# The first block of the last stage ordered by hand, in a fused attention, soft mixture and gated MLP kernel

## The chip, the cores and the metric

The kernel runs on one core of one Trainium2 chip. The metric is the device time of one execution in microseconds (us). A median over runs is given together with the lowest and the highest run. The profile is one further execution with the hardware profiler on.

## The reference

Three layers follow each other. The change lies in the third alone.

```python
# 1: attention with rotary embedding, 4 x 8 heads, 576 tokens, 64 wide -> x of 2304 x 512
attn = softmax(rotate(q) @ rotate(k).T / 8) @ v
# 2: soft mixture of 8 experts with 4 slots each; c: softmax over the 32 slots
x = c @ slot_out                       # c 2304 x 32, slot_out 32 x 512
# 3: MLP, 512 -> 2048 -> 512
h = x @ w_in
out = (h * (1.0 / (1.0 + np.exp(-h)))) @ w_out
```

## The kernel before

The last stage uses that `x @ w_in` is `c @ (slot_out @ w_in)`: it first makes g, the product of the 32 slot rows with w_in, and then needs only 32 rows of contraction for each hidden value. The 2304 tokens are worked in three blocks j of 768, and the 2048 features in 16 chunks k of 128. For one (j, k) the stage does this:

- `hidden(j, k)`: f0 is a matrix product on TensorE (PE) of a chunk of g (`gs`) with the combine weights `cs`, once for each half i of 384 tokens, into a PSUM tile `hps`. Only two such tiles exist (pool `ps_h`, 2 buffers). f1 is the sigmoid on ScalarE (ACT), f2 the product with h on VectorE (DVE), f3 the rounded part `ghi` on ACT, f4 the rest `glo` on DVE. An `hps` tile is free when its f4 is done.
- `products(j, k, i)`: three matrix products of 512 columns (`wo_hi` by `ghi`, `wo_lo` by `ghi`, `wo_hi` by `glo`) for each of six groups of 128 tokens, summed over k in six PSUM tiles `ops`. So a chunk is 18 products of this kind and two of f0.

In block 0 the stage also prepares what the later blocks use. w_out comes from memory as 64-bit words (`w_out_raw`, three buffers in turn). `narrow` makes 32-bit values of a chunk by one instruction on ACT (L143) and two on DVE (L146, L149); `split_hl` then makes `wo_hi` on ACT and `wo_lo` on GpSimd (POOL). Chunks 0, 3, 6 and 10 were converted earlier. `load_wo` issues the load of a later raw chunk on SyncE (SP), and it has to wait until the conversion has read the chunk that was in the same buffer three loads before. `conv_last` converts in the same way the four parts of the last quarter of w_in. g is made in four parts n of four chunks: `g_product(n)` is 32 small products in an `hps` tile and two copies `gh` and `gl` (ACT, DVE), and `g_copy(n, r)` then spreads one chunk of the part by four small DMAs, issued on SP, into `gs`.

The order on the engines: while `tc.manual_schedule()` is open, instructions stand on each engine as the code is written; when `order.close()` has ended it, a scheduler places them. Before, the hand order ends after the hidden chunk 1 of block 0, and the scheduler places all that follows.

The loop over `seq` runs through the 48 pairs (j, k). In step n it works the six `products` of pair n, and after token group i = 2 the `hidden` of pair n + 2. Small jobs are hung on points of the loop by numbers that are 6 n + i: `G_STEPS` says where `g_product` of parts 1 to 3 stands, and `SPREAD` where the first of the four `g_copy` of each part stands (the next three follow 6 apart).

Of the kernel before, what the change touches and what calls it, by code (L numbers as in the profile page):

```python
# [7 lines left out]
F32 = mybir.dt.float32  # L8
# [3 lines left out]
ACTF = mybir.ActivationFunctionType  # L12
ALU = mybir.AluOpType
# [19 lines left out]
TB = 128 * NI  # L33
# [22 lines left out]
QO = (0, 256, 576)  # L56
QN = (256, 320)

G_STEPS = (5, 25, 49)
LOAD_STEP = 28  # L60
SPREAD = (7, 27, 51)
CONV_AT = (2, 5, 8, 9)


@with_exitstack
def attn_softmoe_mlp_kernel(ctx: ExitStack, tc: tile.TileContext, qk, v, cst, phi, w1, w2, w_in, w_out, out):
    nc = tc.nc
    pe, act, dve, pool, sp = nc.tensor, nc.scalar, nc.vector, nc.gpsimd, nc.sync
# [62 lines left out]
    def load_64(src, wp, tag, name):  # L131
        t = wp.tile([128, 1024], U32, tag=tag, name=name)
        sp.dma_start(out=t, in_=src)
        return t.rearrange("p (n t) -> p n t", t=2)

    def narrow(words, out, wp, name, tag="hw", hw=None):
        o = out.bitcast(U32)
        if hw is None:
            hw = wp.tile([128, words.shape[1]], F32, tag=tag, bufs=1, name=name)
        hi = hw.bitcast(U32)  # L140

        def n0():
            act.activation(out=hw, in_=words.bitcast(F32)[:, :, 1], func=ACTF.Prelu, scale=2.0 ** -112, alpha=2.0 ** 32)  # L143

        def n1():
            dve.tensor_scalar(out=o, in0=hi, scalar1=3, scalar2=None, op0=ALU.logical_shift_left)  # L146

        def n2():
            dve.scalar_tensor_tensor(out=o, in0=words[:, :, 0], scalar=29, in1=o, op0=ALU.logical_shift_right, op1=ALU.bitwise_or)  # L149

        return n0, n1, n2

    raw_w, wf_early = {}, {}

    LATE = [k for k in range(16) if k not in W_OUT_EARLY]

    def load_wo(i):
        if i < len(LATE):
            k = LATE[i]
            raw_w[k] = load_64(w_out[128 * k:128 * k + 128], wa, f"w{i % 3}", f"w_out_raw{k}")  # L160
# [3 lines left out]
    def halves(n, i):  # L164
        t = wa.tile([128, 2, 512], F32, tag=f"w{NWA - 2 + i}", name=f"w_in{n}_{i}")
        w_next.update({(n, 2 * i + k): t[:, k] for k in range(2)})
        return t
# [22 lines left out]
    with tc.manual_schedule():  # L190
        with ExitStack() as t1:
# [505 lines left out]
            for p in range(NPAIR):  # L697
# [9 lines left out]
                if p % 4 == 3 and p < NPAIR - 1:  # L707
                    b = p // 4
# [170 lines left out]
            a, b = rot[0], rot[1] = rotary(0), rotary(1)  # L879
# [65 lines left out]
            t = ps_mx.tile([128, 2, 512], F32, tag="mx", name="u_31")  # L945
# [34 lines left out]
            t = ps_mx.tile([128, 2, 512], F32, tag="mx", name="lt3_ps")  # L980
# [6 lines left out]
        def pool2(name, bufs, space=None, st=ctx, **kw):  # L987
            kw.update({"reuse_waits": "tile"}, **({"space": space} if space else {}))
            return st.enter_context(tc.tile_pool(name=name, bufs=bufs, **kw))
# [35 lines left out]
        op = {}  # L1025
# [82 lines left out]
        order = ExitStack()  # L1108
# [38 lines left out]
        t = ps_h.tile([128, 512], F32, tag="h", name="g0_ps")[:, 0:128]  # L1147
# [12 lines left out]
    g2 = pool2("g2", 2, side=left)  # L1160
# [5 lines left out]
    def narrow_wo(k):  # L1166
        w = wf_early[k] = w2p.tile([128, DM], F32, tag="wf", name=f"wf{k}")
        for f in narrow(raw_w.pop(k), w, w2p, f"hwo{k}"):
            f()

    def split_hl(k, w, eng=pool):
        if k in WO_SLOT:
            t = wa.tile([128, 2, DM], F32R, tag=f"w{WO_SLOT[k]}", name=f"wo_hl{k}")
            wo_hi[k], wo_lo[k] = t[:, 0], t[:, 1]
        elif k == WO_TAB:
            t = p_tab.tile([128, 2, S], F32R, tag="tab", name=f"wo_hl{k}")
            wo_hi[k], wo_lo[k] = t[:, 0, 0:DM], t[:, 1, 0:DM]
        else:
            wo_hi[k] = wo.tile([128, DM], F32R, tag=f"hi{k}", name=f"wo_hi{k}")
            wo_lo[k] = wo.tile([128, DM], F32R, tag=f"lo{k}", name=f"wo_lo{k}")  # L1180
        act.activation(out=wo_hi[k], in_=w, func=ACTF.Copy)
        eng.tensor_tensor(out=wo_lo[k], in0=w, in1=wo_hi[k].bitcast(F32), op=ALU.subtract)

    gt, later = {}, []

    def hidden(j, k, between=None):
        ghi = gp.tile([128, 2, TB // 2], F32R, tag="ghi", name=f"ghi{j}_{k}")
        glo = gp.tile([128, 2, TB // 2], F32R, tag="glo", name=f"glo{j}_{k}")
        t, g = {}, {}

        def f0(i):
            t[i] = ps_h.tile([128, TB // 2], F32, tag="h", name=f"hps{j}_{k}_{i}")
            c0 = TB // 2 * i
            pe.matmul(t[i], lhsT=gs2[k // 8][:, 128 * (k % 8):128 * (k % 8) + 128], rhs=cs[j][:, c0:c0 + TB // 2], start=True, stop=True)  # L1194

        def f1(i):
            g[i] = g2.tile([128, TB // 2], F32, tag="g", name=f"g{j}_{k}_{i}")
            act.activation(out=g[i], in_=t[i], func=ACTF.Sigmoid)  # L1198

        def f2(i):  # L1200
            dve.tensor_tensor(out=t[i], in0=t[i], in1=g[i], op=ALU.mult)  # L1201

        def f3(i):
            act.activation(out=ghi[:, i], in_=t[i], func=ACTF.Copy)  # L1204

        def f4(i):
            dve.tensor_tensor(out=glo[:, i], in0=t[i], in1=ghi[:, i].bitcast(F32), op=ALU.subtract)  # L1207

        if between:
            for f, i in ((f0, 0), (f0, 1), (f1, 0), (f2, 0), (f1, 1), (f2, 1)):  # L1210
                f(i)
            copy = between(0)
            f3(0)
            copy()
            for f, i in ((f4, 0), (f3, 1), (f4, 1)):
                f(i)
        elif j == 0:
            f0(0)
            f1(0)
            f2(0)  # L1220

            def rest():
                for f in (f0, f1, f2):
                    f(1)
                def ahead():
                    if k + 1 in LATE:
                        narrow_wo(k + 1)
                        load_wo(LATE.index(k + 1) + 3)
                    elif k in CONV_AT:
                        conv_last(CONV_AT.index(k))  # L1230

                if k > 1:
                    ahead()
                for f in (f3, f4):
                    for i in range(2):
                        f(i)
                if k == 1:
                    ahead()
                else:
                    split_hl(k, wf_early[k])  # L1240
                if k + 1 in LATE and k in CONV_AT:
                    conv_last(CONV_AT.index(k))

            later.append(rest)
        else:
            for i in range(2):
                for f in (f0, f1, f2, f3, f4):
                    f(i)
        gt[j, k] = ghi.rearrange("p a b -> p (a b)"), glo.rearrange("p a b -> p (a b)")

    def conv_last(k):
        if k % 2 == 0:
            halves(3, k // 2)
        words = raw_in[k // 2][:, k % 2].rearrange("p (n t) -> p n t", t=2)
        for f in narrow(words, w_next[3, k], wa, f"hw3_{k}", "w3"):
            f()
# [16 lines left out]
    def g_copy(n, r):  # L1273
        c0 = 512 * (n % 2) + 128 * r
        for q in range(4):
            sp.dma_start(out=gs2[n // 2][32 * q:32 * q + 32, c0:c0 + 128].bitcast(F32), in_=gfull[n][q // 2][32 * r:32 * r + 32].bitcast(F32))
# [8 lines left out]
    seq = [(j, k) for j in range(NBLK) for k in range(16)]  # L1285
# [26 lines left out]
    for i in (2, 3):  # L1312
        load_wo(i)
    hidden(*seq[1])
    later.pop()()
    order.close()
    extra = {}

    def put(x, f):
        extra.setdefault(divmod(x, NI), []).append(f)  # L1320

    for n in range(1, 4):
        put(G_STEPS[n - 1], lambda n=n: g_product(n))
        for r in range(4):
            put(SPREAD[n - 1] + NI * r, lambda n=n, r=r: g_copy(n, r))
    put(LOAD_STEP, lambda: load_last(1))
    for n, (j, k) in enumerate(seq):
        ghi, glo = gt.pop((j, k))
        for i in range(NI):
            if n or i > 3:  # L1330
                products(j, k, i, ghi, glo)
            t = ops[j, i]
            if (n, i) in extra:
                for f in extra.pop((n, i)):
                    f()
            if i == (2 if n else 4) and n + 2 < len(seq):
                hidden(*seq[n + 2])
            elif i == (3 if n else 5) and later:
                later.pop()()
            if k == 15:  # L1340
                o = g2.tile([128, DM], F32, tag="os", bufs=6, name=f"os{j}_{i}")
                if i % 2:
                    dve.tensor_copy(out=o, in_=t)
                else:
                    act.activation(out=o, in_=t, func=ACTF.Copy)
                r0 = TB * j + 128 * i
                sp.dma_start(out=out[r0:r0 + 128], in_=o)
# [46 lines left out]
```

## Time and profile before

| | us |
|---|---|
| median of 3 runs | 557.17 |
| lowest and highest | 556.64, 558.12 |
| the profiled execution, device time | 557.69 |
| its span in the trace | 555.9 |
| TensorE (PE) busy in it | 539.8 |
| VectorE (DVE), ScalarE (ACT) busy | 314.3, 298.6 |

The last stage begins at about 326 us of the span, block 0 ends near 401, and the last matrix product ends at 551.3. A time of the trace counts from the start of the span. The device time holds 1.8 us more than the span.

### The profile page before, as it was taken

Reading aid. Unit: us, or ns where it says so; the run is one execution under the profiler, and the core shown is the slowest. Engines: PE = TensorE matmul, PEld = TensorE weight load, DVE = VectorE, ACT = ScalarE, POOL = GpSimd, SP = SyncE. Lnnn points to the kernel's source line nnn. Section 1 sums busy time; section 2 is a strip of 40 time slices with the busy share of each in tenths; the row PEclk is TensorE's granted clock in tenths of the full one; section 3 lists DMA queues with packets and bytes.
Section 4 is the critical chain, followed back from the end, with each engine's and each line's share of the span. In section 5 each row is a group of like instructions: output and inputs, shape, how many; then the busy total and the mean of one; then the engine's idle time right before and its main releaser. Section 6 shows DMA issues by size and latency. Waiting matters only on the chain.

```text
span 555.9 us, 15287 instructions
## 1 busy us (share of the span) xinstructions
PE 539.8 (97%) x6283; PEld 436.9 (79%) x6283; DVE 314.3 (57%) x826; ACT 298.6 (54%) x582; POOL 113.0 (20%) x105
## 2 busy tenths in 40 slices
PE   8989999999999999999999999999999999999996
PEld 5767898889888989888863457688888888888885
DVE  5767676766656567654130557886454444544442
ACT  3666767656766566664420357666454443533441
POOL 4475433412334323200000032312000000000000
PEclk9999999999999999999999999999999999999999
DMA  8335777555663685753799976361030000300003
GB/s 329 122 101 195 236 263 250 196 183 182 221 222 125 213 284 185 248 191 107 285 340 380 339 297 215 109 223 39 1 114 0 1 0 1 114 2 0 0 1 114
DMA packets 38721, 89.32 MB, mean 161 GB/s; under 512 B 10598, under 2 KB 13948, under 8 KB 36732
## 3 DMA queue, kind: packets, MB, share of 16 engines
q1 hardware_dynamic: 38652, 88.36, 45.7%
q8 instruction: 49, 0.80, 0.6%
q14 instruction: 20, 0.16, 0.1%
HBM read 78.20 MB, written 7.60 MB: 154 GB/s over the span
## 4 chain that ended last, share of the span: by engine, by line
PE 86%; ACT 7%; DVE 4%; issue 3%; ACTq 0%; DVEq 0%
PE ops L1294 11%; PE ops L1296 11%; PE ops L1295 11%; PE u L431 11%; PE st L398 8%; PE psmx L327 4%; PE st_r L411 3%; PE hps L1194 3%; PE xps L459 3%; ACT e L402 3%; PE l L1011 3%; PE l L1032 3%; ACT relu L335 2%; PE u L425 2%; PE psmx L343 2%
## 5 line engine op out<-in xcount | busy, mean ns | idle before, releaser
L1201 DVE TENSOR_TENSOR hps<-hps,g 128x384 f32<-128x384 f32 x96 | 50.6, 562 | 83.3 <-ACT g L1198 83.2
L1198 ACT ACTIVATE g<-hps 128x384 f32<-128x384 f32 x96 | 43.3, 490 | 86.8 <-PE hps L1194 86.7
L348 DVE CUSTOM_DVE_ANT_0 relu<-psmx,relu 128x288 f32<-128x288 f32 x142 | 59.5, 454 | 43.7 <-ACT e L402 38.0
L402 ACT ACTIVATE e<-st 128x512 f32<-128x512 f32 (+1 forms) x128 | 76.4, 650 | 10.4 <-PE st L398 10.3
L431 PE MATMUL u<-v,e 128*64 128x65 f32 x2048 | 80.1, 224 | 0.3 <-ACT e L402 0.3
L1294 PE MATMUL ops<-wo_hi,ghi 128*128 128x512 f32 x198 | 77.9, 394 | 1.5 <-ACT ghi L1204 1.5
L1296 PE MATMUL ops<-wo_hi,glo 128*128 128x512 f32 x198 | 77.6, 392 | 0.0
L1295 PE MATMUL ops<-wo_lo,ghi 128*128 128x512 f32 x198 | 77.2, 390 | 0.0
L431 PEld LDWEIGHTS u<-v,e 128*64 128x64 f32 x2048 | 70.8, 137 | 6.7 <-issue 2.9
L335 ACT ACTIVATE relu<-psmx 128x576 f32<-128x576 f32 x63 | 41.0, 652 | 49.4 <-PE psmx L327 39.7
L277 POOL TENSOR_TENSOR raw<-raw,tab 128x576 f32<-128x576 f32 x28 | 40.5, 1446 | 113.0 <-DMA raw<-in_qk_dram 71.2
L1207 DVE TENSOR_TENSOR glo<-hps,ghi 128x384 fp32r<-128x384 f32 x96 | 50.1, 553 | 4.6 <-ACT ghi L1204 0.7
L1204 ACT ACTIVATE ghi<-hps 128x384 fp32r<-128x384 f32 x96 | 46.0, 492 | 10.5 <-DVE hps L1201 10.3
L1294 PEld LDWEIGHTS ops<-wo_hi,ghi 128*128 128x128 f32 x198 | 37.2, 188 | 9.4 <-ACT ghi L1204 2.5
L1296 PEld LDWEIGHTS ops<-wo_hi,glo 128*128 128x128 f32 x198 | 37.2, 188 | 8.4 <-DVE glo L1207 0.3
L1295 PEld LDWEIGHTS ops<-wo_lo,ghi 128*128 128x128 f32 x198 | 37.2, 188 | 6.3
L274 POOL TENSOR_TENSOR raw<-raw,tab 128x576 f32<-128x576 f32 x28 | 41.9, 1496 | 0.0
L398 PE MATMUL st<-hi 64*128 64x256 f32 (+1 forms) x256 | 39.2, 300 | 0.0
L398 PE MATMUL st<-lo,hi 64*128 64x256 f32 (+1 forms) x256 | 38.2, 293 | 0.0
L398 PE MATMUL st<-hi,lo 64*128 64x256 f32 (+1 forms) x256 | 38.2, 292 | 0.0
L398 PE MATMUL st<-mq,neg_a 64*128 64x256 f32 (+1 forms) x256 | 38.1, 291 | 0.0
L1294 PE MATMUL ops<-wo_hl,ghi 128*128 128x512 f32 x90 | 35.2, 391 | 0.0
(236 smaller groups left out, 993.6 us busy)
## 6 DMA issues: line engine op xcount, KB each, us to landing
w<-in_w_dram SPq DMA_DIRECT2D x64, 512.0 KB
raw<-in_qk_dram SPq DMA_DIRECT2D x14, 1152.0 KB
w_out_raw<-in_w_out_dram SPq DMA_DIRECT2D x16, 512.0 KB
w_in_raw<-in_w_in_dram SPq DMA_DIRECT2D x12, 512.0 KB
v<-in_v_dram SPq DMA_DIRECT2D x16, 325.0 KB
out_dram<-os SPq DMA_DIRECT2D x18, 256.0 KB
w_in<-w_in SPq DMA_DIRECT2D x8, 256.0 KB
w_in_raw<-in_w_in_dram SPq DMA_DIRECT2D x2, 1024.0 KB
```

Source lines behind the costliest of these rows:

```text
L335: act.activation(out=r, in_=pair[:, :, 0:HS], func=ACTF.Relu)
L348: dve.tensor_tensor_reduce(out=r[:, hd], in0=t[hd], in1=r[:, hd], scale=1.0, scalar=-3.0e38, op0=ALU.add, op1=ALU.max, accum_out=mxs[p % 2 ...
L398: pe.matmul(st[:, hd, 0:n], lhsT=a, rhs=b, start=i == 0, stop=i == 3, skip_group_check=True)
L402: act.activation(out=e[:, :, 0:n], in_=st[:, :, 0:n], func=ACTF.Exp, scale=0.125)
L431: pe.matmul(u[q:q + 64, 2 * i + hd], lhsT=e[:, hd, o:o + 64], rhs=x[:, hd], start=n == 0 and i + hd == 0, stop=n == 4, skip_group_check=True)
L1198: act.activation(out=g[i], in_=t[i], func=ACTF.Sigmoid)
L1201: dve.tensor_tensor(out=t[i], in0=t[i], in1=g[i], op=ALU.mult)
L1204: act.activation(out=ghi[:, i], in_=t[i], func=ACTF.Copy)
L1207: dve.tensor_tensor(out=glo[:, i], in0=t[i], in1=ghi[:, i].bitcast(F32), op=ALU.subtract)
L1294: pe.matmul(t, lhsT=a, rhs=wo_hi[k], start=k == 0, stop=False)
L1295: pe.matmul(t, lhsT=a, rhs=wo_lo[k], start=False, stop=False)
L1296: pe.matmul(t, lhsT=b, rhs=wo_hi[k], start=False, stop=k == 15)
```

## The change

Five things change, all in the last stage. The hand order stays open until step n = 14, so it holds for all of block 0. In `hidden` of block 0 the conversions for the next w_out chunk and for w_in stand behind the work of the whole chunk (f0 to f4 for both halves), and `split_hl` of chunk k stands ahead of it; the former split in two pieces (`later`) is gone. The first chunk's first half is worked in 128 and 256 tokens. `hidden` of the third chunk is written after token group 5 of step 0 and not after group 4. Part 3 of g is made at 55 and spread from 57 (49 and 51 before), and `conv_last` runs with chunks 3, 5, 8, 9.

```diff
-G_STEPS = (5, 25, 49)
+G_STEPS = (5, 25, 55)
-SPREAD = (7, 27, 51)
-CONV_AT = (2, 5, 8, 9)
+SPREAD = (7, 27, 57)
+CONV_AT = (3, 5, 8, 9)
...
         if between:
-            for f, i in ((f0, 0), (f0, 1), (f1, 0), (f2, 0), (f1, 1), (f2, 1)):
-                f(i)
+            a, b = slice(0, 128), slice(128, TB // 2)
+            f0(0)
+            f0(1)
+            for w in (a, b):
+                f1(0, w)
+                f2(0, w)
             copy = between(0)
-            f3(0)
+            f3(0, a)
+            f3(0, b)
             copy()
-            for f, i in ((f4, 0), (f3, 1), (f4, 1)):
-                f(i)
+            f4(0, a)
+            f4(0, b)
+            for f in (f1, f2, f3, f4):
+                f(1)
         elif j == 0:
...
+            if k > 1:
+                split_hl(k, wf_early[k])
+            for f in (f0, f1, f2, f3, f4):
+                for i in range(2):
+                    f(i)
+            if k + 1 in LATE:
+                narrow_wo(k + 1)
+                load_wo(LATE.index(k + 1) + 3)
+            if k in CONV_AT:
+                conv_last(CONV_AT.index(k))
...
     hidden(*seq[1])
-    later.pop()()
-    order.close()
...
-            if i == (2 if n else 4) and n + 2 < len(seq):
+            if i == (2 if n else 5) and n + 2 < len(seq):
+                if n == 14:
+                    order.close()
                 hidden(*seq[n + 2])
-            elif i == (3 if n else 5) and later:
-                later.pop()()
```

What this does to the order is read at three places. The first is ACT at the start of the stage, where `g_0_0` is the sigmoid of chunk 0's first half, `g_0_1` that of its second, `gf` the copy of the first part of g. In square brackets stand the semaphores that an instruction waits for. Before:

```order
L1071 ACTIVATE gs_5390<-g_ps 128x128 [waits PE_49]
L1198 ACTIVATE g_0_0_5457<-hps_0_0_5453 128x384 [waits DMAHW5_49,DMAHW1_49,PE_49]
L1198 ACTIVATE g_0_1_5460<-hps_0_1_5455 128x384 [waits PE_49]
L1204 ACTIVATE ghi_0_5451<-hps_0_0_5453 128x384 [waits DMAHW4_49,DMAHW6_49,DMAHW1_49,DVE_49]
L1267 ACTIVATE gf_5480<-g_ps_5463 128x96 [waits PE_49]
L1204 ACTIVATE ghi_0_5451<-hps_0_1_5455 128x384 [waits DVE_49]
```

And now:

```order
L1200 ACTIVATE g_0_0_5457<-hps_0_0_5453 128x128 [waits DMAHW5_49,DMAHW7_49,DMAHW1_49,PE_49]
L1200 ACTIVATE g_0_0_5457<-hps_0_0_5453 128x256 [waits DVE_49]
L1206 ACTIVATE ghi_0_5451<-hps_0_0_5453 128x128 [waits DMAHW6_49,DMAHW4_49,DMAHW7_49,DMAHW1_49,DVE_49]
L1206 ACTIVATE ghi_0_5451<-hps_0_0_5453 128x256
L1259 ACTIVATE gf_5479<-g_ps_5462 128x96 [waits PE_49]
L1200 ACTIVATE g_0_1_5485<-hps_0_1_5455 128x384
L1206 ACTIVATE ghi_0_5451<-hps_0_1_5455 128x384 [waits DVE_49]
```

The second piece of the sigmoid (256 tokens) waits for DVE: in the built program for the multiplication of the first piece, which writes the same `hps` tile. The first piece of `ghi` waits for the multiplication of the second piece. The second half's sigmoid moved behind `ghi` and `gf`.

The second place is PE at the step from chunk 0 to chunk 1. Here `g_ps` is part 1 of g, and it, `hps_2_0` and `hps_2_1` take the two `hps` buffers in turn. Before:

```order
L1296 MATMUL ops_5_5556<-wo_hi_5447,glo_0_5452 128x512
L1294 MATMUL ops_0_5486<-wo_hi_5500,ghi_1_5521 128x512
L1295 MATMUL ops_0_5486<-wo_lo_5501,ghi_1_5521 128x512
L1294 MATMUL ops_1_5505<-wo_hi_5500,ghi_1_5521 128x512
L1194 MATMUL hps_2_0_5551<-cs_5318,gs_5390 128x384
L1296 MATMUL ops_0_5486<-wo_hi_5500,glo_1_5522 128x512
L1295 MATMUL ops_1_5505<-wo_lo_5501,ghi_1_5521 128x512
L1264 MATMUL g_ps_5560<-w_in_0_5276,so 32x128 x8
```

And now:

```order
L1288 MATMUL ops_5_5552<-wo_hi_5447,glo_0_5452 128x512
L1256 MATMUL g_ps_5556<-w_in_0_5276,so 32x128 x8
L1256 MATMUL g_ps_5556<-w_in_1_5278,so 32x128 x8
L1195 MATMUL hps_2_0_5583<-cs_5318,gs_5390 128x384
L1195 MATMUL hps_2_1_5585<-cs_5318,gs_5390 128x384
L1286 MATMUL ops_0_5490<-wo_hi_5504,ghi_1_5525 128x512
```

The part of g and both halves of chunk 2 moved ahead of all the products of chunk 1.

The third place is chunk 12 of block 0, on DVE and on SP. `wf_6066` (before) and `wf_6065` (now) is chunk 12 of w_out in conversion, `gl` the copy of part 3 of g. DVE before:

```order
L146 TENSOR_SCALAR wf_6066<-hwo_6067 128x512
L1201 TENSOR_TENSOR hps_9_0_5933<-hps_9_0_5933,g_9_0_5935 128x384
L149 SCALAR_TENSOR_TENSOR wf_6066<-w_out_raw_5852,wf_6066 128x512
L1201 TENSOR_TENSOR hps_9_1_5945<-hps_9_1_5945,g_9_1_5947 128x384
L1207 TENSOR_TENSOR glo_9_5932<-hps_9_0_5933,ghi_9_5931 128x384
L1207 TENSOR_TENSOR glo_9_5932<-hps_9_1_5945,ghi_9_5931 128x384
L146 TENSOR_SCALAR wf_6114<-hwo_6115 128x512
L149 SCALAR_TENSOR_TENSOR wf_6114<-w_out_raw_5901,wf_6114 128x512
L1271 TENSOR_TENSOR gl_5992<-g_ps_5974,gh_5991 128x128
```

And now:

```order
L1263 TENSOR_TENSOR gl_6040<-g_ps_6022,gh_6039 128x128
L1203 TENSOR_TENSOR hps_11_0_6051<-hps_11_0_6051,g_11_0_6055 128x384
L1203 TENSOR_TENSOR hps_11_1_6053<-hps_11_1_6053,g_11_1_6057 128x384
L1209 TENSOR_TENSOR glo_11_6047<-hps_11_0_6051,ghi_11_6046 128x384
L1209 TENSOR_TENSOR glo_11_6047<-hps_11_1_6053,ghi_11_6046 128x384
L146 TENSOR_SCALAR wf_6065<-hwo_6066 128x512
L149 SCALAR_TENSOR_TENSOR wf_6065<-w_out_raw_5856,wf_6065 128x512
L1203 TENSOR_TENSOR hps_12_0_6099<-hps_12_0_6099,g_12_0_6103 128x384
```

Chunk 12 of w_out was converted around chunk 9's work, and is now converted behind chunk 11's. SP stands in the same order before and now; these are its rows now, where `w_out_raw_6070` is the load of the last raw chunk (15), into the buffer that held raw chunk 12, and the four DMAs behind it are the first spread of part 3, that is the g of chunk 12:

```order
L133 DMA w_out_raw_6070<-in_w_out_dram 128x1024 [waits DMAHW0_49,DVE_49,Activation_49]
L1268 DMA gs_5508<-gh_6039 32x128 [waits DMAHW1_49]
L1268 DMA gs_5508<-gh_6039 32x128 [waits DMAHW2_49]
L1268 DMA gs_5508<-gl_6040 32x128 [waits DMAHW3_49]
L1268 DMA gs_5508<-gl_6040 32x128 [waits DMAHW4_49]
```

The load waits for the conversion of chunk 12 on DVE (the L149 row above), and the four copies stand behind the load in the queue.

## Rows read from the trace of the kernel before

**Rows 1.** The page, busy time and share of the span of each engine

```profile
PE 539.8 (97%) x6283; PEld 436.9 (79%) x6283; DVE 314.3 (57%) x826; ACT 298.6 (54%) x582; POOL 113.0 (20%) x105
```

**Rows 2.** Stretches: length, busy per engine (count), granted clock, DMA share, GB/s

```profile
400.00:540.00 140.00, 140.00 (x631) 117.24 (x630) 68.81 (x133) 60.94 (x133) 0.00 (x0) 1.00 0.06 23
```

**Rows 3.** What PE waited for from 320 to 556: us, times, longest

```profile
PE ops L1294 <- ACT ghi L1204: 1.5, 3, 0.7
PE hps L1194 <- DVE glo L1207: 0.7, 1, 0.7
```

**Rows 4.** Timeline of PE: start, us, instruction, [idle before, releaser]

```profile
330.30 0.50 PE L1294 MATMUL ops<-wo_hi,ghi 128*128 128x512 f32 x1 [0.73 <-ACT ghi L1204]
...
334.19 0.51 PE L1194 MATMUL hps<-cs,gs 128*128 128x384 f32 x2
...
336.23 0.50 PE L1294 MATMUL ops<-wo_hi,ghi 128*128 128x512 f32 x1 [0.15 <-ACT ghi L1204]
...
337.76 1.08 PE L1264 MATMUL g_ps<-w_in,so 128*32 128x128 f32 x32
...
351.85 0.50 PE L1294 MATMUL ops<-wo_hi,ghi 128*128 128x512 f32 x1 [0.57 <-ACT ghi L1204]
...
380.28 0.33 PE L1194 MATMUL hps<-cs,gs 128*128 128x384 f32 x1
...
384.76 0.33 PE L1194 MATMUL hps<-cs,gs 128*128 128x384 f32 x1
```

**Rows 5.** The page, groups of instructions: busy us, mean ns of one

```profile
L1201 DVE TENSOR_TENSOR hps<-hps,g 128x384 f32<-128x384 f32 x96 | 50.6, 562 | 83.3 <-ACT g L1198 83.2
L1198 ACT ACTIVATE g<-hps 128x384 f32<-128x384 f32 x96 | 43.3, 490 | 86.8 <-PE hps L1194 86.7
```

**Rows 6.** Timeline of ACT

```profile
327.50 0.28 ACT L1071 ACTIVATE gs<-g_ps 128x128 fp32r<-128x128 f32 x1
...
339.18 0.63 ACT L1181 ACTIVATE wo_hi<-wf 128x512 fp32r<-128x512 f32 x1
```

**Rows 7.** Timeline of DVE

```profile
332.82 0.56 DVE L1072 TENSOR_TENSOR gs<-g_all,gs 64x384 fp32r<-64x384 f32 x1 [0.29 <-ACT gs L1071]
...
336.21 1.02 DVE L1207 TENSOR_TENSOR glo<-hps,ghi 128x384 fp32r<-128x384 f32 x2
337.23 0.43 DVE L146 TENSOR_SCALAR wf<-hwo 128x512 uint32<-128x512 uint32 x1
...
338.47 0.68 DVE L149 SCALAR_TENSOR_TENSOR wf<-w_out_raw,wf 128x512 uint32<-128x512 uint32 x1
...
339.59 0.28 DVE L1271 TENSOR_TENSOR gl<-g_ps,gh 128x128 fp32r<-128x128 f32 x1
...
349.09 1.67 DVE L149 SCALAR_TENSOR_TENSOR wf<-w_out_raw,wf 128x512 uint32<-128x512 uint32 x1
```

**Rows 8.** Timeline of the DMA issues on SP's queue

```profile
332.76 6.78 SPq L133 DMA_DIRECT2D w_out_raw<-in_w_out_dram  x3
339.63 1.24 SPq L1276 DMA_DIRECT2D gs<-gh  x2
340.93 1.21 SPq L1276 DMA_DIRECT2D gs<-gl  x2
...
376.06 1.15 SPq L1276 DMA_DIRECT2D gs<-gh  x2
377.30 1.17 SPq L1276 DMA_DIRECT2D gs<-gl  x2
```

**Rows 9.** Stretches of 0.25 us; the last two numbers are DMA share and GB/s

```profile
379.25:379.50 0.25, 0.25 (x3) 0.21 (x2) 0.25 (x2) 0.10 (x1) 0.00 (x0) 1.00 0.07 16
379.50:379.75 0.25, 0.25 (x3) 0.21 (x2) 0.25 (x1) 0.25 (x1) 0.00 (x0) 1.00 0.00 0
```

**Rows 10.** Stretches of 0.5 us ahead of the last stage; granted clock is third from the end

```profile
290.00:290.50 0.50, 0.50 (x4) 0.28 (x4) 0.43 (x4) 0.00 (x0) 0.00 (x0) 0.50 1.07 414
...
293.00:293.50 0.50, 0.50 (x8) 0.12 (x4) 0.00 (x0) 0.00 (x0) 0.00 (x0) 0.82 1.03 377
```

More of the change, by code (lines that the diff above doesn't have):

```diff
@@ L1182, in split_hl @@
         eng.tensor_tensor(out=wo_lo[k], in0=w, in1=wo_hi[k].bitcast(F32), op=ALU.subtract)
-    gt, later = {}, []
+    gt = {}
     def hidden(j, k, between=None):
@@ L1189, in hidden @@
         t, g = {}, {}
+        whole = slice(0, TB // 2)
         def f0(i):
@@ L1194, in f0 @@
             pe.matmul(t[i], lhsT=gs2[k // 8][:, 128 * (k % 8):128 * (k % 8) + 128], rhs=cs[j][:, c0:c0 + TB // 2], start=True, stop=True)
[L1196 to L1207, printed above, removed]
@@ L1209, in hidden, with f1, f2, f3 @@
-        if between:
-            for f, i in ((f0, 0), (f0, 1), (f1, 0), (f2, 0), (f1, 1), (f2, 1)):
-                f(i)
+        def f1(i, w=whole):
+            if i not in g:
+                g[i] = g2.tile([128, TB // 2], F32, tag="g", name=f"g{j}_{k}_{i}")
+            act.activation(out=g[i][:, w], in_=t[i][:, w], func=ACTF.Sigmoid)
+        def f2(i, w=whole):
+            dve.tensor_tensor(out=t[i][:, w], in0=t[i][:, w], in1=g[i][:, w], op=ALU.mult)
+        def f3(i, w=whole):
+            act.activation(out=ghi[:, i, w], in_=t[i][:, w], func=ACTF.Copy)
@@ L1212, in hidden, with f4 @@
+        def f4(i, w=whole):
+            dve.tensor_tensor(out=glo[:, i, w], in0=t[i][:, w], in1=ghi[:, i, w].bitcast(F32), op=ALU.subtract)
+        if between:
+            a, b = slice(0, 128), slice(128, TB // 2)
[4 more added lines that the diff above has]
+                f2(0, w)
             copy = between(0)
-            f3(0)
+            f3(0, a)
+            f3(0, b)
             copy()
-            for f, i in ((f4, 0), (f3, 1), (f4, 1)):
-                f(i)
+            f4(0, a)
+            f4(0, b)
+            for f in (f1, f2, f3, f4):
+                f(1)
@@ L1217, in hidden @@
         elif j == 0:
[L1218 to L1242, printed above, removed]
@@ L1244, in hidden @@
-            later.append(rest)
+            if k > 1:
[8 more added lines that the diff above has]
+                conv_last(CONV_AT.index(k))
         else:
```

## Prediction

> **What bounds the kernel now.** I read the page first. TensorE is busy for 97% of the span [rows 1], and in blocks 1 and 2 of the last stage for the whole of the stretch, at a granted clock of 1.00 [rows 2]. So only what TensorE waits for, or its clock, can move the end, and a wait added ahead of that stretch is not made up later. Next I read what it waits for in the last stage: 1.5 us in three pieces for `ghi`, 0.7 us once for `glo` [rows 3]. The timeline places them: 0.73 at the first product of the stage, 0.15 and 0.57 later [rows 4], and the 0.7 follows the last of these. All of this lies between 329 and 354 us. It is the most that a better order could give back: 0.73 + 0.15 + 0.57 + 0.70 = 2.15 us, 0.4% of the time.
>
> **The change, part by part.** The number of matrix products stays; only waits change.
>
> *The first half of chunk 0 in two pieces.* Before, three steps stand between the f0 product and the first `ops`: sigmoid, product, copy. Now they are five steps in a row, since the second sigmoid piece waits for the multiplication of the first, and `ghi` for the multiplication of the second. ACT takes 0.28 for 128 columns [rows 6] and 0.49 for 384 [rows 5], DVE 0.28 [rows 7] and 0.56 [rows 5]; between them I estimate 0.38 and 0.42 for 256. Before: 0.49 + 0.56 + 0.49 and two handovers of about 0.04, 1.62. Now: 0.28 + 0.28 + 0.38 + 0.42 + 0.28 and four handovers, 1.80. **+0.2** (0 to +0.4).
>
> *The g of chunks 1 to 3.* The first f0 of chunk 1 needs the DVE subtraction that before ended at 332.82 + 0.56 = 333.38 [rows 7], 0.8 us ahead of the product at 334.19 [rows 4]. Now all four steps of chunk 0's second half, 0.49 + 0.56 + 0.49 + 0.56 with handovers 2.2 us, start only after `ghi` and `gf` on ACT, 0.45 after the first `ops`, at about 330.75. They end near 332.95; then come the two conversion instructions, 0.43 + 0.68 [rows 7], and the subtraction, 0.56: 334.6. TensorE, 0.2 late, is there at 334.4. **+0.2** (0 to +0.6).
>
> *Chunk 0 to chunk 1.* How soon an `hps` buffer comes back is read from chunk 1: f0 at 334.19 [rows 4], the first `glo` done at about 336.77, the second at 337.23 [rows 7], so 2.58 and 3.04 us. Between f0 of chunk 1 and part 1 of g TensorE now has 0.35 + six products of 0.23, 1.73 us. It waits 2.58 − 1.73 = **0.85**. After part 1 (1.01 us, the spacing in [rows 4]) and the first half of chunk 2 it is free at 3.80. The second half needs the buffer of part 1, so `gl`, and that stands on DVE behind the conversion of chunk 2: 3.04 + 0.43 + 0.68 + 0.28 and handovers, 4.45. It waits **0.65**.
>
> *Chunk 2 to 3.* Here `wo_hi` (0.63 [rows 6]) stands on ACT ahead of chunk 2's sigmoid and needs that same conversion. The sigmoid starts some 0.25 us after the second f0, against 0.37 after its own f0 before; so the buffers come back 2.45 and 2.9 us after that f0. TensorE has 0.17 + nine products, 2.24. It waits about **0.25** and then **0.3** for the other half. From chunk 4 on there are 18 products, 4.48 us from f0 to f0 (380.28 to 384.76 [rows 4]), for a round of 3.04; I find no further wait for a buffer.
>
> *What falls away.* The waits of 0.15, 0.57 and 0.70 belong to the scheduler's order. In it conversions stood between a chunk's steps, and one took 1.67 us where others take 0.68 [rows 7]. Together −1.4.
>
> The early part: 0.2 + 0.2 + 0.85 + 0.65 + 0.55 − 1.42 = **+1.0 us**. If the waits for buffers are half of this, −0.2; if conversions are stretched as in the 1.67 row, +2.0.
>
> *Chunk 12.* This is the largest term. SP works its queue in order. The load of raw chunk 15 waits for the conversion of w_out chunk 12, and the four copies of chunk 12's g stand behind it. Before, that conversion was done around chunk 9, and part 3 of g, made earlier, left SP from 376.06 [rows 8], 8.7 us ahead of f0 at 384.76 [rows 4]. Now the conversion comes behind chunk 11's f0 to f4, and chunk 12's f0 follows chunk 11's by 4.48. From chunk 11's f0 on: both `glo` done after 3.04, conversion 0.43 + 0.68 and handovers, 4.18. Then SP: in [rows 8] a row of three loads, the last held for a conversion, ends at 339.54; the conversion ended at 338.47 + 0.68 = 339.15 [rows 7], and the first copy starts at 339.63, so 0.48 after it. The fourth copy starts 1.9 later (the second of the pair at 340.93). The fourth of the copies that started at 376.06 started near 377.9, and its bytes moved until 379.50 at the latest [rows 9], 1.5 us on. Sum: 4.18 + 0.48 + 1.9 + 1.5 = 8.06. TensorE stands there from 4.48: **+3.6 us**. Bounds: 3.0 (bytes there 1.0 after the issue, handovers nothing) and 5.0 (the conversion stretched by 1.0, bytes 0.4 later). Behind that wait stand f0 of chunk 12 and all later products, so nothing covers it.
>
> The Trainium skill (DMA: Bandwidth & Descriptors, the two cost components) gives a DMA a fixed 2.0 us plus bytes. By it the fourth copy lands 2.04 after its start, and the wait is estimated at 4.1 us. The rows show bytes, not the semaphore, so they bound it from below only.
>
> For chunks 5, 8, 9 and 10 the copies stand in the same way behind a load and a conversion, but two chunks ahead: 8.06 us against 8.96. That is 0.9 us to spare, so no wait in my sum; it is the next thing to go late.
>
> *The clock.* The granted clock fell to 0.50 at 290 and came back near 293.2 [rows 10], the lower level of 1.2 GHz, after a stretch of small matrix products without any long stop. It stayed up over 0.57 + 0.70 us of waiting within 2.5 us. A full stop of 3.6 us is nearer to the first. If it falls, half of some 3.3 us is lost, less what lies inside the stop: 0 to 1.7, I take **+1.0**. The Trainium skill (TensorE: Matmul & The Clock Gate, on HAM oscillation) also tells of kernels whose clock falls in each wait for a DMA.
>
> **Sum.** 1.0 + 3.6 + 1.0 = +5.6. The profiled execution took 557.69 (span 555.9 and 1.8 around it), which gives 563.3. The median of the runs is 0.5 lower, 557.17, and on that base I forecast **562.8 us**.
>
> **The rivals.**
> 1. *The clock stays up in the stop.* All else as above: 557.17 + 1.0 + 3.6 = 561.8. For it: the waits of rows 3 cost no clock. Against it: rows 10.
> 2. *The copies are not late (not slower).* If the load of raw chunk 15 does not hold the queue, because the copies pass it or the conversion is done one chunk earlier than the written order says, the four copies land about 4.5 us ahead of their use. Only the early term stays: 557.17 + 1.0 = 558.2, +0.2%, within the measurement. The point from which it decides: all four copies landed within 4.48 us of chunk 11's f0. For it: before, nothing waited for these copies. Against it: in [rows 8] the queue stood 6.78 us over three loads until a conversion was done.
> 3. *The order gives what its early waits hold.* If the buffers come back within TensorE's 1.7 to 2.2 us, the early waits do not arise and −1.4 stays; with the copies in time 555.7. Rows 4 and 7 speak against it: 2.58 was measured there with nothing in between.
> 4. *More copies are late.* If a copy lands a further 1.2 us later, chunks 5, 8, 9 and 10 wait some 0.3 each and chunk 12 1.2 more: 562.8 + 2.4 = 565.2.
>
> **How the numbers follow.** Forecast 0.47, rival 1 0.33, rival 2 0.08, rival 3 0.05, rival 4 0.07. A difference under 0.3% of the time, 1.7 us, can hardly be told from none here. Forecast and rivals 1 and 4 are slower by more than that: 0.87. Rival 2 is no change that can be told: 0.08. Rival 3 is about 1.5 us faster, at the edge, and stands for faster: 0.05. The range for 8 in 10 goes from 560.2 (rival 1 with 0.4 for the early term and 2.6 for the late) to 565.0 (the forecast with 5.0 for the late one and the clock at 1.7).
>
> **What would show it.** Right: TensorE waits once for 3 to 4 us in block 0 near 385 to 390, and SP's queue shows a load of `w_out_raw` that waits for L149 just ahead of it; three to five waits for `glo` or `gl` between 334 and 343; the granted clock at 0.50 for some us behind the long wait. Blocks 1 and 2 without a wait. Wrong: no wait for DMA at chunk 12, or copies that start on SP before L149 of chunk 12 is done. The early waits are wrong if part 1 of g starts right after the products of chunk 0. The sum is off by size if the first `ops` starts before 330.3.

## The result, and the profile after

| | before | after |
|---|---|---|
| median, us | 556.97 (4 runs) | 564.78 (4 runs) |
| lowest and highest | 556.64, 558.12 | 563.26, 566.94 |
| profiled execution, its span | 557.69, 555.9 | 566.94, 564.9 |

The ratio of after to before is 1.0138, 95% interval 1.0104 to 1.0172: slower by 7.8 us. The forecast of 562.8 (560.2 to 565.0) names the right side, and its range holds the time; the forecast itself is 2.0 us under the median.

The profiled execution of after is 2.2 above its median, because its last stage began late: the first f0 starts at 330.56, against 326.5 to 328.2 in nine of the eleven profiles of this study, ahead of every changed instruction. To keep that apart I compare the **stage length**, from the first f0 to the start of the last matrix product:

| | first f0 | last product | stage length | against before |
|---|---|---|---|---|
| before | 328.15 | 550.90 | 222.75 | |
| after | 330.56 | 560.61 | 230.05 | +7.30 |

Page of after, busy time of the engines; it answers to [rows 1]:

```profile
PE 543.7 (96%) x6283; PEld 438.8 (78%) x6283; DVE 312.7 (55%) x828; ACT 299.9 (53%) x584; POOL 114.0 (20%) x105
```

The count of matrix products is the same; busy time grows by 3.9, in the main since the same products take longer at a lower clock, here and ahead of the stage. What TensorE waits for in the last stage of after (the three longest); it answers to [rows 3]:

```profile
PE hps L1195 <- DMA gs<-gl: 5.6, 2, 3.9
PE ops L1286 <- ACT ghi L1206: 0.9, 1, 0.9
PE g_ps L1256 <- DVE glo L1209: 0.7, 1, 0.7
```

A line that was not there before leads the list: two waits for the small copies of g, 5.6 us in all, where the forecast had one of 3.6. The timeline of PE places them, as in [rows 4]:

```profile
332.90 0.50 PE L1286 MATMUL ops<-wo_hi,ghi 128*128 128x512 f32 x1 [0.93 <-ACT ghi L1206]
...
337.15 0.62 PE L1195 MATMUL hps<-cs,gs 128*128 128x384 f32 x2 [0.19 <-DVE gs L1072]
337.61 0.39 PE L1286 MATMUL ops<-wo_hi,ghi 128*128 128x512 f32 x1
...
338.76 0.40 PE L1288 MATMUL ops<-wo_hi,glo 128*128 128x512 f32 x1
339.90 1.08 PE L1256 MATMUL g_ps<-w_in,so 128*32 128x128 f32 x32 [0.74 <-DVE glo L1209]
340.91 0.44 PE L1195 MATMUL hps<-cs,gs 128*128 128x384 f32 x1
341.72 0.44 PE L1195 MATMUL hps<-cs,gs 128*128 128x384 f32 x1 [0.37 <-DVE gl L1263]
...
343.83 0.39 PE L1288 MATMUL ops<-wo_hi,glo 128*128 128x512 f32 x1
344.28 0.91 PE L1195 MATMUL hps<-cs,gs 128*128 128x384 f32 x2
345.03 0.39 PE L1286 MATMUL ops<-wo_hi,ghi 128*128 128x512 f32 x1
...
368.14 0.51 PE L1195 MATMUL hps<-cs,gs 128*128 128x384 f32 x2
...
372.36 0.39 PE L1288 MATMUL ops<-wo_hi,glo 128*128 128x512 f32 x1
374.42 0.59 PE L1195 MATMUL hps<-cs,gs 128*128 128x384 f32 x2 [1.68 <-DMA gs<-gl]
...
384.64 0.51 PE L1195 MATMUL hps<-cs,gs 128*128 128x384 f32 x2
...
393.15 0.98 PE L1195 MATMUL hps<-cs,gs 128*128 128x384 f32 x2 [3.89 <-DMA gs<-gl]
393.93 0.63 PE L1286 MATMUL ops<-wo_hi,ghi 128*128 128x512 f32 x1
394.36 0.63 PE L1287 MATMUL ops<-wo_lo,ghi 128*128 128x512 f32 x1
```

The row at 368.14 is the f0 of chunk 8, that at 374.42 chunk 9, that at 393.15 chunk 12. A reading aid: the idle time in brackets counts from the modelled end of the product before, 0.39 after its start, while in steady work the next product starts 0.23 after it. So each wait behind such a product costs about 0.16 more than its bracket. The products at 393.93 and 394.36 stand 0.43 apart in place of 0.23: half speed. Stretches of after around them, and of blocks 1 and 2 (length, PE busy and count, granted clock, DMA share, GB/s); they answer to [rows 2, 10]:

```profile
290.00:293.00 3.00, 3.00 (x23) 0.55 1.05 395
293.00:296.00 3.00, 3.00 (x16) 0.50 1.04 388
...
369.00:372.00 3.00, 3.00 (x15) 1.00 0.95 363
...
390.50:391.50 1.00, 0.00 (x0) 1.00 0.99 390
...
392.00:393.00 1.00, 0.00 (x0) 0.84 0.11 25
393.00:396.00 3.00, 2.85 (x7) 0.50 0.12 27
...
410.00:550.00 140.00, 140.00 (x631) 1.00 0.06 23
```

The clock is at 0.50, the 1.2 GHz level, from 393 to 396, behind the stop at chunk 12. Blocks 1 and 2 have no wait, as forecast. At 290 the clock fell in both profiles, but came back near 297 here and 293.2 before: at half clock for some 6.8 us here and 3.4 before, which by estimate makes 1.7 of the 2.4 us by which the stage begins later. The chain of waits of after ahead of chunk 12 (start, us, what):

```profile
388.27 0.70 DVE wf L149
...
389.03 0.33 SPq L133
...
389.41 0.51 SPq L1268
...
391.24 1.78 DMA gs<-gl
393.02 0.14 issue
393.15 0.98 PE hps L1195 x2
```

It reads as the forecast said: the conversion of w_out chunk 12 ends, SP is released for the load (L133), the four copies (L1268) follow, and f0 starts when the last has landed. SP's queue of after, as in [rows 8], shows chunk 9's copies too:

```profile
366.50 0.53 SPq L187 DMA_DIRECT2D w_in_raw<-in_w_in_dram  x1
368.09 0.34 SPq L133 DMA_DIRECT2D w_out_raw<-in_w_out_dram  x1
368.48 1.15 SPq L1268 DMA_DIRECT2D gs<-gh  x2
369.67 1.22 SPq L1268 DMA_DIRECT2D gs<-gl  x2
...
383.35 6.01 SPq L133 DMA_DIRECT2D w_out_raw<-in_w_out_dram  x2
389.41 1.15 SPq L1268 DMA_DIRECT2D gs<-gh  x2
```

The second load of the pair at 383.35 is held until the conversion is done and leaves SP at 389.36. The first copy, at 389.41, then starts later than f0 was due (389.09), so the hold is enough for a stop. While the copies follow, that load's 0.5 MB still move (DMA share 0.99 from 390.5 to 391.5). The copies of chunk 9 follow a load of 1 MB (L187) and one of 0.5 MB, and the DMA engines are busy for 0.95 of the stretch from 369 to 372, just ahead of the stop.

### The profile page after: what moved, and what is told of

The parts are those of the page before. It is cut to its first block, busy times and chain, and to the rows that moved or that the text cites. A ratio compares the mean times of both kernels' runs of the same rounds, so it can differ in the third digit from the quotient of the medians.

```text
span 564.9 us, 15284 instructions
## 1 busy us (share of the span) xinstructions
PE 543.7 (96%) x6283; PEld 438.8 (78%) x6283; DVE 312.7 (55%) x828; ACT 299.9 (53%) x584; POOL 114.0 (20%) x105
## 4 chain that ended last, share of the span: by engine, by line
PE 83%; ACT 8%; DVE 4%; issue 3%; DMA 1%; SPq 1%; ACTq 0%; DVEq 0%
PE u L431 11%; PE ops L1286 10%; PE ops L1288 10%; PE ops L1287 10%; PE st L398 8%; PE psmx L327 4%; PE hps L1195 3%; PE st_r L411 3%; PE l L1011 3%; PE xps L459 3%; ACT e L402 3%; PE l L1032 3%; ACT relu L335 2%; PE u L425 2%; PE psmx L343 2%
## 5 line engine op out<-in xcount | busy, mean ns | idle before, releaser
L1203 DVE TENSOR_TENSOR hps<-hps,g 128x384 f32<-128x384 f32 (+1 forms) x97 | 49.7, 557 | 90.3 <-ACT g L1200 90.3
L1200 ACT ACTIVATE g<-hps 128x384 f32<-128x384 f32 (+1 forms) x97 | 42.2, 485 | 80.7 <-PE hps L1195 80.4
L1206 ACT ACTIVATE ghi<-hps 128x384 fp32r<-128x384 f32 (+1 forms) x97 | 46.1, 489 | 12.9 <-DVE hps L1203 12.9
L1209 DVE TENSOR_TENSOR glo<-hps,ghi 128x384 fp32r<-128x384 f32 (+1 forms) x97 | 49.2, 548 | 5.5 <-ACT ghi L1206 1.2
```

Source lines behind the costliest of these rows:

```text
L1200: act.activation(out=g[i][:, w], in_=t[i][:, w], func=ACTF.Sigmoid)
L1203: dve.tensor_tensor(out=t[i][:, w], in0=t[i][:, w], in1=g[i][:, w], op=ALU.mult)
L1206: act.activation(out=ghi[:, i, w], in_=t[i][:, w], func=ACTF.Copy)
L1209: dve.tensor_tensor(out=glo[:, i, w], in0=t[i][:, w], in1=ghi[:, i, w].bitcast(F32), op=ALU.subtract)
```

## The experiments

The theory: (a) chunk 12 stops because its copies stand on SP behind one load that waits for a conversion; (b) the clock falls because TensorE stands there; (c) chunk 9 stops because its copies are held likewise and their bytes also queue behind 1.5 MB of loads; (d) the early order costs and gives about the same. Ratios are to the kernel before, run on the same chip.

| kernel | median, us (runs) | ratio, 95% interval | stage length |
|---|---|---|---|
| changed, once more | 565.31 (4) | 1.0156 (1.0134 to 1.0179) | 231.03 |
| part 3 of g early | 559.48 (8) | 1.0048 (1.0031 to 1.0065) | 225.40 |
| before, part 3 of g late | 557.34 (10) | 1.0012 (0.9995 to 1.0030) | 222.75 |
| one load behind the copies | 558.11 (10) | 1.0020 (0.9999 to 1.0041) | 225.38 |
| stop filled | 563.57 (4) | 1.0122 (1.0086 to 1.0158) | 228.71 |
| 1 MB load later | 568.47 (1) | one run, no interval | 234.56 |
| all loads behind the copies | 556.63 (12) | 1.0002 (0.9986 to 1.0018) | 222.60 |
| the same, first chunk in one piece | 556.12 (12) | 0.9990 (0.9975 to 1.0005) | 221.91 |
| the same, f0 and g later | 553.63 (6) | 0.9947 (0.9930 to 0.9963) | 220.50 |

**The changed kernel once more.**

> The changed kernel once more, beside the next three on one chip. Theory: 1.0138 of before again (564.7 us), the stop at chunk 12 of 3.9 us and the clock at 0.50 for some 3 us behind it in the profile, since both follow from the order; the stop at chunk 9 between 1.5 and 2.5 us. Rival: the fall of the clock is a matter of chance in each execution and is missing here (563.3).

The same stops came, at chunk 12 4.02 and at chunk 9 1.62. The clock fell again, during the stop, and for longer; stretches of this run (columns as above):

```profile
387.00:389.00 2.00, 0.00 (x0) 0.68 0.65 235
389.00:394.00 5.00, 4.37 (x11) 0.50 0.12 28
```

Its stage is 0.98 longer than that of after with nearly the same waits, so the price of the fall varies by about 1 us from one execution to the next.

**Part 3 of g early.** On the changed kernel:

```diff
-G_STEPS = (5, 25, 55)
+G_STEPS = (5, 25, 49)
-SPREAD = (7, 27, 57)
+SPREAD = (7, 27, 51)
```

> The changed kernel with part 3 of g and its copies at the old steps (49 and 51), all else as changed. Theory: the stop at chunk 12 (3.9 us) comes from the four copies that stand on SP behind a load that waits for the conversion of chunk 12; one chunk earlier they have 0.9 us to spare. So the stop goes, and with it the clock fall (1.45 us): 564.8 - 3.9 - 1.45 = 559.4 us, 1.004 of the kernel before, no wait for a DMA at chunk 12, granted clock 1.00 throughout block 0. Rival A (the conversion behind chunk 11 alone makes it): the stop stays, about 564.8. Rival B (the clock falls in this place whatever TensorE waits for): stop gone, clock still at 0.50 for some 3 us, 560.9. The stop of 1.7 at chunk 9 should stay in all cases.

559.48 for 559.4. From 340 to 410 PE waits for one thing only, the copies of chunk 9, and the clock stays up:

```profile
PE hps L1195 <- DMA gs<-gl: 2.5, 1, 2.5
```

Rivals A and B fall: the conversion behind chunk 11 is still there, and neither the stop nor the fall of the clock is. The stop at chunk 9 is longer than the 1.7 expected, though its copies leave SP at the same point as in after, 0.34 behind the f0 of chunk 8. Their bytes came some 0.9 later; why is not shown.

**Before, part 3 of g late.** The same two lines the other way round, on the kernel before, with its scheduler's order:

```diff
-G_STEPS = (5, 25, 49)
+G_STEPS = (5, 25, 55)
-SPREAD = (7, 27, 51)
+SPREAD = (7, 27, 57)
```

> The kernel before (scheduler's order) with part 3 of g and its copies at the late steps (55 and 57) alone. Theory: the late steps hurt only together with conversions that are done late; in this order the conversion of chunk 12 is done early, so the copies are late by nothing: within 0.5 us of before, 557.0 to 557.5, clock 1.00. Rival A (the late steps alone make the stop): 557.0 + 3.9 + 1.45 = 562.3, with a wait for a DMA at chunk 12.

No difference that can be told; the stage length is that of before to 0.01 us, and PE is busy for 50.00 of 50 us from 360 to 410. So neither half of the change makes the stop alone: late copies do no harm where the conversion is early, and a conversion behind chunk 11 does none where the copies are early.

**One load behind the copies.** On the changed kernel:

```diff
+    put(SPREAD[2] + 1, lambda: load_wo(11))
...
-                load_wo(LATE.index(k + 1) + 3)
+                if k != 11:
+                    load_wo(LATE.index(k + 1) + 3)
```

> The changed kernel with one DMA moved: the load of raw w_out chunk 15 is issued right behind the four copies of chunk 12's g and no longer ahead of them; late steps and conversions stay. Theory (the copies are held on SP by this one load): the stop at chunk 12 and the clock fall go, 564.8 - 5.35 = 559.4, 1.004 of before. Rival C (the copies are late because part 3 of g itself is made late, or because their bytes are slow): the stop stays nearly whole, above 563. Rival B (clock falls anyway): 560.9. The stop at chunk 9 stays.

558.11: 1.3 better than expected. From 340 to 410 the stop at chunk 9, 1.54 here, is all that is left; chunk 12 has none with part 3 of g as late as ever. That is the hold on SP, shown with one DMA moved. Rival C falls. In this profile the clock fell elsewhere, behind the 0.92 wait at the first product of the stage (columns as above):

```profile
329.00:332.00 3.00, 3.00 (x12) 0.51 0.03 11
```

So a wait under 1 us can be followed by it too, in some executions: after and five other profiles with the same wait of 0.92 or 0.93 kept 1.00 there. The load's bytes moved behind the copies together with its place on SP; the first copy's late start in after (389.41) is what tells the hold from the bytes.

**The stop filled.** On the changed kernel, for the first f0 of chunk 12 alone, 20 products (`fill`) into the tile that f0 then overwrites:

```diff
+            for _ in range(fill):
+                pe.matmul(t[i], lhsT=gs2[1][:, 384:512], rhs=cs[j][:, c0:c0 + TB // 2], start=True, stop=True)
             pe.matmul(t[i], lhsT=gs2[k // 8][:, 128 * (k % 8):128 * (k % 8) + 128], rhs=cs[j][:, c0:c0 + TB // 2], start=True, stop=True)
```

> The changed kernel with 20 matrix products of 128x384 whose result is overwritten, put in the stop at chunk 12 (about 3.4 us of work on an otherwise empty TensorE). Theory (the clock falls because TensorE stands still): the wait for the copies shrinks to a few tenths of a us as these products take its place, f0 of chunk 12 starts at the same time, and the granted clock stays 1.00 behind it: 564.8 - 1.45 = 563.3 us. Rival B (the fall has another cause, such as the work done before): clock at 0.50 as before, 564.8. If the products take longer than the stop the time goes up by what they run over.

PE's timeline, and the stretches behind it (columns as above):

```profile
385.56 3.66 PE L1197 MATMUL hps<-cs,gs 128*128 128x384 f32 x20
389.72 0.59 PE L1198 MATMUL hps<-cs,gs 128*128 128x384 f32 x2 [0.51 <-DMA gs<-gl]
```

```profile
389.00:393.00 4.00, 3.49 (x17) 1.00 0.11 27
393.00:397.00 4.00, 4.00 (x20) 1.00 0.10 25
```

f0 of chunk 12 starts 62.65 after the first f0 of the stage, 62.59 in after: the stop is as long as it was. The clock stays at 1.00 and the stage is 1.34 shorter (expected 1.45). The medians differ by 1.2, and their intervals overlap, so they do not prove it. The mean clock of each run goes the same way: two of the four runs of the filled kernel held 1.00 and took 562.1, while none of the eight runs of the changed kernel shows more than 0.997, and none is under 563.2. So at this place the fall comes from standing still.

**The 1 MB load later.** On the changed kernel `LOAD_STEP` 34 in place of 28.

> The changed kernel with the 1 MB load of raw w_in issued one step behind the copies of chunk 9 (step 34 in place of 28), so that these copies have no large load but the 0.5 MB one ahead of them, and are held on SP as before. Theory: at chunk 9 the hold on SP leaves the copies 0.9 us to spare, and the 1.5 MB that move ahead of their bytes make the fourth land 3.98 us after its issue in place of 1.8: without the 1 MB the wait at chunk 9 goes or falls under 0.4 us. Rival (the hold on SP alone makes it): 1.5 us or more stays at chunk 9. By the way, in either case the conversion of the third quarter of w_in behind chunk 8 must now wait for its load, which delays the sigmoids of chunk 9 and makes a wait of 1 to 3 us for ghi or glo at chunk 9 or 10; the stop at chunk 12 stays. So the time says little here, the waits do: about 564 to 566.

f0 of chunk 9 starts at 369.57, 4.45 after that of chunk 8: no wait, with SP held just as in after and the 0.5 MB load still ahead of the copies. The DMA engines are nearly idle just ahead of it (columns as above):

```profile
368.00:369.00 1.00, 1.00 (x6) 1.00 0.18 44
```

So (c) needs the bytes of the 1 MB load. What the load was moved into is the next wait, on ACT and then PE:

```profile
373.71 0.66 ACT L143 ACTIVATE hw<-w_in_raw 128x512 f32<-128x512 f32 x1 [5.51 <-DMA w_in_raw<-in_w_in_dram]
```

```profile
369.57 0.51 PE L1195 MATMUL hps<-cs,gs 128*128 128x384 f32 x2
...
377.26 0.84 PE L1195 MATMUL hps<-cs,gs 128*128 128x384 f32 x2 [3.08 <-DVE glo L1209]
```

The conversion of w_in waits 5.51 for its load and holds the sigmoids of chunk 9 behind it; chunk 10 waits 3.08, just above the 1 to 3 expected, and the clock fell there as well (0.57 from 378 to 382). Behind the stop at chunk 12, 3.97, it fell again and for longer than in after (0.51 from 392 to 399). So the time came out at 568.47, in one run, above the 564 to 566 expected.

**All loads behind the copies.**

```diff
-                load_wo(LATE.index(k + 1) + 3)
+                loads.append(LATE.index(k + 1) + 3)
...
+            if i == 4 and loads:
+                load_wo(loads.pop())
```

> The changed kernel with every load of a raw w_out chunk in block 0 issued behind the copies of its step and not ahead of them; all else, the 1 MB load of raw w_in too, as changed. Theory: at chunk 12 as when the one load was moved; at chunk 9 the copies are issued some 1.6 us earlier and have only the 1 MB load ahead of them and no longer the 0.5 MB load, so their bytes are there before 372.7: no wait for a DMA in block 0. 564.8 - 3.9 - 1.45 - 1.7 = 557.7 us, 1.0015 of before. Rival D (the 1 MB load alone delays the copies of chunk 9): a wait of 1 us or more stays there, 558.7 to 559.4.

From 340 to 410 PE has no wait that carries a bracket, and the time is that of before. SP's queue shows the copies of chunk 9 (from 361.50) against f0 at 370.08:

```profile
358.94 0.53 SPq L187 DMA_DIRECT2D w_in_raw<-in_w_in_dram  x1
361.11 0.34 SPq L133 DMA_DIRECT2D w_out_raw<-in_w_out_dram  x1
361.50 1.15 SPq L1268 DMA_DIRECT2D gs<-gh  x2
```

My expectation was right in the time and wrong in the way: the copies still have both loads ahead of them, and they are there because they are issued 8.6 us ahead of f0, not 1.6 earlier than before. In after it was 4.1 (368.48 to the 372.59 at which f0 was due). With the run before this: the hold and the bytes together make the stop at chunk 9, and taking away either ends it.

**First chunk in one piece.** On the last kernel, the order of before for the first chunk:

```diff
-            for w in (a, b):
-                f1(0, w)
-                f2(0, w)
+            for f, i in ((f1, 0), (f2, 0), (f1, 1), (f2, 1)):
+                f(i)
...
-            for f in (f1, f2, f3, f4):
-                f(1)
+            for f, i in ((f4, 0), (f3, 1), (f4, 1)):
+                f(i)
```

> The kernel with all loads behind the copies, and the first chunk's first half again in one piece of 384 tokens with both sigmoids ahead of the first copy, as before the change. Theory: the first product of the stage waits 0.73 in place of 0.92 and the first f0 of chunk 1 nothing in place of 0.2: about 0.4 us less than with the pieces, 557.3. Rival E (the pieces gain time): 0.2 or more slower than with them, 557.9, the first product waiting more than 0.92.

```profile
332.18 0.50 PE L1281 MATMUL ops<-wo_hi,ghi 128*128 128x512 f32 x1 [0.73 <-ACT ghi L1206]
...
336.05 0.51 PE L1195 MATMUL hps<-cs,gs 128*128 128x384 f32 x2
```

The first product waits 0.73 again (0.92 with the pieces) and the first f0 of chunk 1 nothing. The stage is 0.69 shorter, 0.4 expected. The two waits account for 0.66 of it, since that f0 costs 0.46 with the pieces, of which the bracket shows 0.19 (next section). The medians differ by 0.5 with intervals that overlap, so the time alone does not prove it; the waits do. Rival E falls.

**f0 and g later.** On the last kernel:

```diff
-G_STEPS = (5, 25, 55)
+G_STEPS = (6, 30, 60)
-SPREAD = (7, 27, 57)
+SPREAD = (7, 31, 61)
...
-            if i == (2 if n else 5) and n + 2 < len(seq):
+            if 6 * n + i == 6 * ahead - 5 and ahead < len(seq):
...
-                hidden(*seq[n + 2])
+                hidden(*seq[ahead])
+                ahead += 1
```

> As the last, and from chunk 2 on each chunk's f0 stands two (for the first) or five products of 0.7 us later in the written order, the three parts of g one to five products later (steps 6, 30, 60, copies from 7, 31, 61). Theory: between two uses of an hps buffer TensorE then always has more work than the 2.6 to 3.0 us that a buffer takes to come back, so the waits for glo and gl (0.74, 0.38) and the small one behind them go; left are 0.73 at the first product, some 0.3 for ghi at chunk 1 and 0.27 for gs. The waits of block 0 fall from 2.4 (before) to about 1.3: 557.0 - 1.1 - 0.4 for halves of f0 that stand together = 555.5 us, 0.997 of before. Rival F (in the later blocks, which the scheduler orders, a late f0 makes new waits): 557 or more, TensorE not busy for the whole of 410 to 540.

553.63 us, 0.9947 of before (0.9930 to 0.9963): it beats both kernels, and is 1.9 under the 555.5 expected. About 0.6 of that is the base, since I counted from 557.0 and before took 556.45 beside it. All that PE waits for from 320 to 545:

```profile
PE ops L1281 <- ACT ghi L1206: 0.7, 1, 0.7
PE hps L1195 <- DVE gs L1072: 0.3, 1, 0.3
```

Later blocks have no wait (PE busy 130.00 of 130 from 410 to 540), so rival F falls. The stage is 2.25 shorter than before, and the first wait of 0.73 is still in it. So the order of block 0 held at least that much; the prediction had sized it at 1.42 of waits that fall away, and called 2.15, the first wait included, the most that a better order could give back. Of the 2.25, this step itself gave 1.41 (221.91 to 220.50); f0 and g were moved together, and what each gave is not shown.

## Why the prediction was right, and where its sizes were off

The side was right, and so were the place and the mechanism of the largest term; a second stop, at chunk 9, was priced at nothing. The terms, against spacings in the trace of after where a wait has to be given whole:

| step of the prediction | forecast | measured | from |
|---|---|---|---|
| first half of chunk 0 in two pieces | +0.2 | +0.20 | 0.93 less 0.73 |
| first f0 of chunk 1 | +0.2 | 0.46 | 0.19 + 0.16, and 337.61 less 337.15 + 0.35 |
| part 1 of g | 0.85 | 0.91 | 339.90 less 338.76 + 0.23 |
| second half of chunk 2 | 0.65 | 0.63 | 341.72 less 340.91 + 0.18 |
| chunk 2 to 3 | 0.55 | 0.62 | 345.03 less 343.83 + 0.23 + 0.35 |
| what falls away | −1.4 | about −3.0 | the −0.15 of the next row less the five above, 2.82 |
| early part, net | +1.0 | −0.15 | loads behind copies less before, 222.60 − 222.75 |
| chunk 9 | 0 (0.9 to spare) | 1.83 | 374.42 less 372.36 + 0.23 |
| chunk 12 | +3.6 | 4.06 | 393.15 less 384.64 + 4.45 |
| clock | +1.0 | 1.34 | after less stop filled |
| sum | +5.6 | 7.1 | against 7.30 in the stage length |

*The early order.* Each wait that the change adds came where it was said, and four of the five within 0.1 us; the first f0 of chunk 1 cost 0.46 for 0.2, mostly unseen in its bracket. Of the three to five waits for `glo` or `gl` that were forecast two carry a bracket; the delay from chunk 2 to 3 shows in the spacing alone. The step that was off is "what falls away": I took the brackets of before, 0.15 + 0.57 + 0.70. A bracket leaves out some 0.16 of each wait, and delays too short for a bracket are not listed. One such delay stands in every chunk: with both halves of f0 side by side a chunk takes 4.45 us (368.14 to 372.36 + 0.23), and 4.48 before [rows 4], some 0.4 over twelve chunks by estimate. The last experiment's order without these waits bounds the term from below: before stands 2.25 above it. How the rest up to 3.0 divides is not shown.

*Chunk 12.* From chunk 11's f0 at 384.64: conversion done at 388.96 (4.32, forecast 4.18), first copy 0.45 later (0.48), fourth 1.83 after it (1.9), landed 1.78 later (1.5), 0.13 to f0. The sum of 8.51 against 8.06 makes 0.45 of the 0.46. The Trainium skill (DMA: Bandwidth & Descriptors, the two cost components) gave an estimate of 4.1 for this wait, by a fixed 2.0 us that the page fits for DMAs issued from GpSimd. The copies here are issued on SP, and the chain shows 1.78 for the fourth, about midway between 2.0 and my 1.5. So the 4.1 meets the measured 4.06 in part by luck: the conversion was done 0.14 later than either sum had it.

*Chunk 9.* This is the step that failed: "0.9 us to spare, so no wait in my sum". The hold on SP was right: the fourth copy's issue began near 370.3. But I let it land 1.5 later as an idle DMA does. Here 1.5 MB of loads had been issued just ahead, and f0 could start only at 374.42, some 4 us after that issue. Rival 4 named the place and the effect (copies later by 1.2, chance 0.07), and not what makes it or that only chunk 9 stands so: the 1 MB load comes once. The median, 564.8, lies nearer to that rival's 565.2 than to the forecast, but by other terms: it had 0.3 at each of four chunks and 1.2 more at chunk 12. The row that I should have read is the 1 MB load at step 28, one step group ahead of chunk 9's copies. The Trainium skill (DMA: Bandwidth & Descriptors, queues, rings and completion order) says that each DMA engine consumes the descriptors of a ring in ring order; the run with the load moved agrees, since the wait of 1.68 was gone once the load's bytes stood behind the copies.

*The clock.* The fall came as forecast, by standing still as the filled stop shows, and cost 1.34 in after, inside 0 to 1.7; the second profile shows it can be about 1 us more, which is above that range. Rival 1 (clock stays up, 0.33) did not happen in either profile of the changed kernel. Rivals 2 and 3 did not happen: the copies did not pass the held load.

Against the forecast, then: early −1.15, chunk 9 +1.83, chunk 12 +0.46, clock +0.34, together +1.5 of the 2.0 between the two medians' forecast and measure. The rest is within the spread of the runs. That the median stands inside the range, 0.2 under its upper end, is partly luck: the early part came out 1.15 lower than forecast and hid most of the 1.83 at chunk 9.

## What to carry to other kernels

On SP a load that waited some 5 us for its buffer held the four copies behind it, so put a transfer with a waiting reader ahead of a load that must first wait for a buffer; that one reordering gave back all that this change cost. When a copy has little time to spare, look at the bytes issued just ahead of it, not only at its place in the queue. With two PSUM buffers in turn, count the work between two uses against the time that a buffer takes to come back (here 2.6 to 3.0 us) and spread the uses until it fits: that took 1.41 us off the stage here, while the finer split of the first chunk cost 0.69.

## What the runs showed of the hardware

- A copy of 16 KB within the chip landed 1.78 us after its issue, with a load of 0.5 MB issued 2.2 us ahead of it still moving in part. Behind loads of 1.5 MB issued up to 4 us earlier the same copy landed some 4.0 us after its issue in after, and some 4.8 in the run with part 3 of g early.
- The granted clock fell to 0.50 in or behind stops of 3.9 and 4.0 us in two of two profiles of the changed kernel, and at both long stops (3.1 and 4.0) of the run with the 1 MB load later. Behind the five stops of 1.5 to 2.5 us at chunk 9 it stayed at 1.00. Once it fell behind a wait of 0.92 us which in six other profiles cost no clock. With 20 matrix products of 384 columns in the stop at chunk 12 it stayed at 1.00.
- The fall at 290 us, among small products and at a place that no kernel here changed, is not in every execution: before, after and the run with the first chunk in one piece show it, the other eight profiles do not. The stage began at 328.15, 330.56 and 330.03 with it, 326.5 to 328.0 without. So the two profiles of the changed kernel differ by 3.6 us (330.56 and 326.94) ahead of the place under study, and a length from a fixed mark in the program is the better measure of a change.
